# Attention and mixture of experts on one core: a reordered opening, later sums of V, and part of the early routing off VectorE

## The chip, the core and the metric

The kernel runs on one core of one Trainium2 chip. The metric is the time of one launch in microseconds (us), and of several runs the median. One further execution was taken by the hardware profiler; its trace is what the sections below quote.

## The reference, cut to what matters

```python
q_bits = (einsum('bhsd,dk->bhsk', q, proj) > 0)          # 6 sign bits per row of q, the same for k
mask   = q_bucket[:, :, :, None] == k_bucket[:, :, None, :]
scores = where(mask, q @ k.T / sqrt(64), -1e9)
attn   = exp(scores - scores.max(-1)); attn /= attn.sum(-1) + 1e-09
x      = (attn @ v) as 3072 tokens x 512                 # 4 batches, 8 heads, 768 rows, 64 columns
flat   = (x @ w_gate).flatten()                          # 3072 x 8 logits
for idx in argsort(-flat):                               # greedy: best logit first
    give token idx//8 to expert idx%8, unless the token has one or the expert has its 384
out    = per expert e: relu(x[mask_e] @ w1[e]) @ w2[e]   # 512 -> 1024 -> 512
```

## The kernel before, in words

There are 32 heads, taken in 8 groups of four; a group is two pairs of heads, and 128 partitions hold one pair (64 columns each). Every f32 operand is split into a f16 high half and a low half, so that TensorE multiplies in f16 and keeps the precision.

For each head TensorE works through three things. **Score passes** (`S_pass`, L233): for each of six blocks of 128 query rows, two matmuls against all keys, from the high halves and six rows of scaled sign bits, and one VectorE reduction (L241) for the row's maximum. Three maxima at a time are turned into a row (`m_rows`, L243: three short matmuls and one ScalarE step, L248), which becomes one more row of the operand `qa`; `qa` and `ka` hold the high halves, the sign bits and this row, and `qb` and `kb` the other halves. **Scores, transposed** (`ST`, L252): for each of six blocks of 128 keys, in two halves of 384 queries, matmuls L257 and L258 and an exponential on ScalarE (L259) into `pt`. **The product with V** (`AV`, L264), four steps behind: `pt`'s upper 16 bits against V's high and low half (L272, L273), and its low half `lo` (L274), which GpSimd or VectorE makes by a subtraction (L262). For rows whose bucket is empty the sum of V is needed (`sumv`, `sumw`, L194 to L213): matmuls of a column of ones against V's high and low halves (L203), a copy, a second matmul (L209) and a VectorE step into `wf`, with which the head's last product (L278, L279) is taken.

The main loop has 192 steps, one for each head and key block, in two half-steps each. What else a half-step does is fixed by hand in a table, `AP` (L20): `P1`, `P2`, `P3`, `P4` give, for group 1, 2, 3 and the later ones, the half-steps of the high halves (`cast`, L123), the low halves (`sub`, L129), the sign bits (`bits`, L131), the load of V and the sums of V (entry 18); `SU` is the half-step of group 0's sums, `SW` how much later `sumw` follows `sumv` in the later groups; `S` is the line by which score passes run ahead of the scores; `PAT`, `E0`, `E1` say which of a head's six `lo` go to VectorE. `MV` says when SP issues a group's moves into `qa`, `ka`, `qb`, `kb` (`moves`, L165) and, among them, the loads of the next group's q and k.

The **opening** is written out in the string `OPS`: its entries up to the first `|` run in that order ahead of the loop, and those behind belong to half-step 0, 1, and so on. A letter names a step (L319): `b` the projection of head 0's signs (`tbits`), `s` a score pass, `B` the sign bits of head 1 and of the pair of heads 2 and 3, `D` their two DMAs to head 1, `m` the row of maxima, `e` a first half of scores, `v` and `x` high and low half of V, `u` the low halves of pair 1, `r` and `l` head 0's and 1's other halves, `d` and `f` the moves of pair 1 (`dm`, L146, `dm2`, L158), `c` a cast, `C` copies into the second set of buffers, `w` dummy matmuls that keep TensorE busy. `DW[0]` dummies of 512 columns come before anything else. Steps of an engine are issued in the order of the program, so a step that waits holds up all that stand behind it on its engine.

In group 0's `bits` head 1 is read from XT with 64 of the 128 partitions and the pair from the loaded group with all 128; the result is scaled by 8192 on VectorE (L144), in later groups on ScalarE (`bscale`, L145).

After half of batch 3's attention, the **early routing** begins: the logits of the first three batches are known, and `early` (L536) hands out steps one by one, every four half-steps from half-step 307 (`EA`). For the first 18 of 24 columns of tokens, `best` (L485) finds each token's largest logit `m`, the expert it belongs to (`eq` times the weights `wt`, L495, then a maximum `mxu`), a sortable key, its first digit `E` and a one-hot of the expert (`OH`, L502). Three `compare` steps (L507) then set digits of six columns each against a table of 128 thresholds (L510). These run on VectorE, between the reductions of the score passes and the `lo` that fall to it.

The step that ends the early routing's part is followed by rounds of counting (from 395 us) and by the experts' matrix products, in which the change touches nothing.

## Time and profile before

| | |
|---|---|
| three runs | 734.71, 735.23 and 735.5 us, median 735.23 |
| profiled execution | 734.54 us, of which the trace's span is 732.8 |
| TensorE matmul busy | 673.7 us (92%) |
| VectorE busy | 519.3 us (71%) |
| ScalarE busy | 470.1 us (64%) |
| GpSimd busy | 525.4 us (72%) |
| mean granted TensorE clock | 0.97 |
| DMA | 93.58 MB in 39952 packets |

In the rows PE is TensorE's matmuls, PEld its weight loads, DVE VectorE, ACT ScalarE, POOL GpSimd and SP the queue that issues most DMAs. A row of a timeline gives the start in us from the span's start, the duration, the engine, the line, the operation, what it writes and reads, shapes and types, and in brackets how long the engine stood idle before and what ended that. A granted clock of 1.00 is TensorE's full speed, 2.4 GHz, and 0.50 half of it, 1.2 GHz. The attention loop ends at some 395 us. Shares over the whole span mix stages, so stages are read apart.

### The profile page before, as it was taken

To read this page: it belongs to the slowest core of one execution; us is meant where nothing else is said; L and a number is where in the kernel's file an instruction comes from. 1 tells how busy PE (TensorE), PEld (TensorE's weight loads), DVE (VectorE), ACT (ScalarE), POOL (GpSimd) and SP (SyncE) were. 2 spreads that over 40 slices of the span, in tenths; PEclk is the share of its full clock that TensorE was granted. 3 is DMA by queue.
4 is the path that set the end of the run, shared out by engine and by line. 5 is a ranking of instruction groups with operands and counts; after the bars stand their busy time and mean duration, and the time that the engine had idled before them with its cause. 6 is when DMAs were issued, how large, how long until landed. Compare 5 with 4: busy or idle time off the path is not lost. (4 is left out here: it accounts for less than half of the span.)

```text
span 732.8 us, 19247 instructions
## 1 busy us (share of the span) xinstructions
PE 673.7 (92%) x7865; PEld 433.4 (59%) x7865; DVE 519.3 (71%) x1124; ACT 470.1 (64%) x886; POOL 525.4 (72%) x486
## 2 busy tenths in 40 slices
PE   8899989999999999998997599989898989899995
PEld 2566656767767677676675464545454555545552
DVE  5868876878877878788965688697878787843120
ACT  7678776778978788776662172927373645556650
POOL 8589959998988979886772446575756473867761
PEclk9999999999999999999997599999999999999998
DMA  7638572726636255430000344435352526172601
GB/s 194 173 93 229 141 190 50 204 69 134 180 93 165 80 151 158 89 81 23 24 24 23 110 165 147 156 138 179 127 175 98 205 88 229 55 277 58 258 29 43
DMA packets 39952, 93.58 MB, mean 128 GB/s; under 512 B 4548, under 2 KB 30520, under 8 KB 37816
## 3 DMA queue, kind: packets, MB, share of 16 engines
...
q8 instruction: 61, 1.00, 0.6%
...
## 5 line engine op out<-in xcount | busy, mean ns | idle before, releaser
L262 POOL TENSOR_TENSOR lo<-pt 128x768 f16<-128x768 f32 x143 | 229.7, 1621 | 40.6 <-ACT pt L259 33.0
L259 ACT ACTIVATE pt<-pst 128x384 f32<-128x384 f32 x384 | 181.1, 491 | 72.9 <-PE pst L258 63.3
L241 DVE TENSOR_REDUCE m<-pss 128x1 f16<-128x770 f32 x192 | 182.0, 957 | 51.8 <-PE pss L239 50.6
L257 PE MATMUL pst<-qa,ka 128*128 128x384 f16 x384 | 126.1, 329 | 7.3 <-ACT qa L248 4.0
L258 PE MATMUL pst<-qb,kb 128*128 128x384 f16 x384 | 125.8, 328 | 0.0
L274 PE MATMUL psv<-vh,lo 128*128 128x65 f16 x1152 | 121.7, 194 | 3.2 <-POOL lo L262 3.2
L273 PE MATMUL psv<-vl,pt 128*128 128x64 f16 x1152 | 121.9, 193 | 0.0
L272 PE MATMUL psv<-vh,pt 128*128 128x65 f16 x1152 | 121.9, 195 | 0.0
L272 PEld LDWEIGHTS <-pt 128*128 128x128 bf16 x1152 | 107.3, 98 | 11.2 <-issue 3.5
L273 PEld LDWEIGHTS <-pt 128*128 128x128 bf16 x1152 | 106.3, 99 | 8.0 <-issue 0.2
L274 PEld LDWEIGHTS <-lo 128*128 128x128 f16 x1152 | 106.3, 98 | 3.5 <-POOL lo L262 3.5
L239 PE MATMUL pss<-ka,qa 128*128 128x385 f16 x384 | 95.0, 330 | 0.4 <-DVE m L241 0.3
L757 ACT ACTIVATE wh<-wf 128x1024 f16<-128x1024 f32 x64 | 67.0, 1051 | 36.6 <-DMA wf<-in_w_dram,zwidx 34.3
L775 POOL TENSOR_TENSOR wl<-wf,wh 128x512 f16<-128x512 f32 x76 | 85.9, 1147 | 0.0
L818 PEld LDWEIGHTS <-wh 128*128 128x128 f16 x512 | 47.9, 98 | 33.4 <-issue 3.4
L830 PEld LDWEIGHTS <-hh 128*128 128x128 f16 x384 | 36.2, 98 | 40.7 <-issue 3.2
L833 ACT ACTIVATE o<-po 128x512 f32<-128x512 f32 x24 | 14.3, 595 | 70.7 <-PE po L830 60.4
L766 ACT ACTIVATE wf<-wf 128x1024 f32<-128x1024 f32 x55 | 58.0, 1055 | 1.0
L262 DVE TENSOR_TENSOR lo<-pt 128x768 f16<-128x768 f32 x49 | 56.8, 1159 | 1.5 <-ACT pt L259 1.0
L821 DVE SCALAR_TENSOR_TENSOR hl<-px,hh 128x384 f16<-128x384 f32 x64 | 34.6, 551 | 30.6 <-ACT hh L820 29.9
L820 ACT ACTIVATE hh<-px 128x384 f16<-128x384 f32 x64 | 31.0, 484 | 37.6 <-PE px L818 34.0
L818 PE MATMUL px<-xh,wh 128*128 128x384 f16 x256 | 53.6, 326 | 1.1 <-DVE xl L794 0.8
...
## 6 DMA issues: line engine op xcount, KB each, us to landing
...
```

The lines of the kernel that those rows point to most:

```text
L239: T.matmul(ps[:,hf,0:HK],QA[u][:,j,qc*128:qc*128+128],KA[u][:,j,hf*HK:hf*HK+HK],start=True,stop=True)
L241: V.tensor_reduce(M6[h][:,qc:qc+1],ps[:,:,0:HK],axis=AX.XY,op=ALU.max,negate=True)
L257: T.matmul(ps[:,0:384],KA[u][:,j,kr],QA[u][:,j,r],start=True,stop=False)
L258: T.matmul(ps[:,0:384],KB[u][:,j,kr],QB[u][:,j,r],start=False,stop=True)
L259: A.activation(PT[h,kc][0][:,r],ps[:,0:384],AF.Exp,scale=0.125)
L262: eng.tensor_tensor(l,p,p.bitcast(BF)[:,1::2],op=ALU.subtract)
L272: T.matmul(av[:,c,:],ph[:,r],VH[u][:,j,kc,:],start=(kc==0 and c==0),stop=False,skip_group_check=True)
L273: T.matmul(av[:,c,0:64],ph[:,r],VL[u][:,j,kc,:],start=False,stop=False,skip_group_check=True)
L274: T.matmul(av[:,c,:],l[:,r],VH[u][:,j,kc,:],start=False,stop=False,skip_group_check=True)
L757: s.nc.scalar.mul(h[:,r],f[:,r],WSC)
L775: for _ in range(n): s.nc.gpsimd.tensor_tensor(*s.pend.pop(0)[1],op=ALU.subtract)
L818: T.matmul(p[:,0:384],a[:,o:o+128],b[:,d],start=n==0,stop=n==11)
```

## The change

In words:

- *Loads.* The second half of the first rows (`first(1,64)`) is loaded ahead of group 0's pair 1 and V.
- *Sign bits of the opening.* Head 1's are taken with all 128 partitions, so that four column groups run with the same number of rows. The scaling by 8192 is now ScalarE's (`a0`).
- *Order.* `OPS` is written anew: eight dummies of 512 columns instead of five, three score passes ahead of the key bits `B0`, and the first row of maxima, `m0`, right behind them; the low halves of pair 1 (`u0`, `u1`) move ahead of it, and the loads of group 1's q and k (`L0`, `L1`) ahead of pair 1's moves `d0`; V's high and low halves and `m1`, `m2` shift; a copy of one number of `ka` by GpSimd (`g0`) makes that engine wait for the key signs of head 0.
- *Score passes.* `S` goes from [7, 30] to [7, 7].
- *Sums.* Group 0's `sumv` moves from half-step 13 to 15 with `sumw` 2 behind instead of 3; group 1's from 46 to 50, group 2's from 72 to 74, and `sumw` in all later groups from 4 to 9 half-steps behind.
- *Low halves.* Heads 4, 7, 8 and 10 send one more of their six `lo` to VectorE (`XL`).
- *Early routing.* For the first 18 columns the product with `wt` moves to GpSimd, and the experts `mxu` and the digits `E` are copied through TensorE (a matmul with the identity, `lift`) into a bank of PSUM, from which the one-hot and the three comparisons read them. The identity `identb` is made earlier for that.

The diff, cut to its core:

```diff
- S=[7, 30],
- DW=[5, 0, 0, 0, 384],
+ S=[7, 7],
+ DW=[8, 0, 0, 0, 384],
...
- SW=4,
+ SW=9,
+ XL={4:[0,3,5],7:[1,4],8:[0,3,5],10:[0,3,5]},
...
- SU=13,
- OPS='b0 i3 i2 t0 b1 w5 r0 r2 w4 s0 w4 C1 r1 t1 c1 s1 B0 c0 D0 w2 w1 s4 w5 s2 s3 r3 v2 w5 v0 l0 l1 C0 m0 s5 w3 s6 r5 w2 l3 e0 e1 d0 u0 u1 s7 v1 l2 w0 m1 e2 | s8 | x0 | w0 | x1 s9 | r4 s10 | | | s11 m2 v3 f0 | x3 | | x2 | m3 | | | | | |')
+ SU=15,
+ OPS='b0 i3 i2 t0 w2 b1 w3 r0 r2 s0 w2 s1 C1 C0 r1 t1 c1 w4 s2 c0 w3 g0 l0 l1 u0 u1 B0 m0 a0 D0 s3 L0 L1 w2 e0 s4 d0 r3 l3 v2 v0 e1 w2 s5 e2 r5 l2 m1 s6 | s7 | x0 | s8 | v1 x1 | s9 | r4 s10 m2 | | s11 v3 f0 | x3 | | x2 m3 | | | | | |')
...
-    first(0,0); first(0,64); first(1,0)
+    first(0,0); first(0,64); first(1,0); first(1,64)
     for w,src in ((0,qT),(1,kT)): SY.dma_start(LD[0][w][:,1],src[0][:,1])
     SY.dma_start(LD[0][2],vv[0])
-    first(1,64)
...
-                    T.matmul(ps[32*w:32*w+32,hf,0:384],pr[0:64],(qd,kd)[w][0:64,1,hf*384:hf*384+384],start=True,stop=True,tile_position=(0,32*w))
+                    T.matmul(ps[32*w:32*w+32,hf,0:384],pr,(qd,kd)[w][:,1,hf*384:hf*384+384],start=True,stop=True,tile_position=(0,32*w))
...
-        if G==0: V.tensor_scalar(bt[r],bt[r],8192.0,None,op0=ALU.mult)
...
+        e=lambda k: ST(0,k,0),C=lambda n: copies((QA,KA)[n]),w=lambda n: warm(n,DW[4]),a=lambda n: bscale(0),
+        g=lambda n: G_.tensor_copy(tick,KA[0][64:65,0,0:1]))
...
-    add(AP['WS'],wsplit); add(AP['SU'],sumv,0); add(AP['SU']+3,sumw,0)
+    add(AP['WS'],wsplit); add(AP['SU'],sumv,0); add(AP['SU']+2,sumw,0)
...
-            if G==1 or w==2: add(p[19+w],load,G,w)
+            if w==2: add(p[19+w],load,G,w)
...
-            lambda: V.tensor_tensor(eq[:,r],eq[:,r],wt,op=ALU.mult),
+            lambda: W.tensor_tensor(eq[:,r],eq[:,r],wt,op=ALU.mult),
...
-            lambda: V.tensor_tensor(OH[:,r],bc(mxu),wt,op=ALU.is_equal)]
+            lambda: V.tensor_tensor(OH[:,r],s.lift(ps,mxu[:,r])[:,:,None].to_broadcast([128,n,8]) if ps else bc(mxu),wt,op=ALU.is_equal)]
+
+    def lift(s,ps,a):
+
+        g=ps()[:,0:a.shape[1]]
+        s.nc.tensor.matmul(g,s.identb,a,start=True,stop=True)
+        return g
...
+            if b==nb-2: todo.append(lambda a=a: s.compare(s.Z["cmp"][0],0,s.lift(ps,s.Z["E"][:,0,a:a+6]),a,a+6,a))
+            else: todo.append(lambda a=a: s.compare(s.Z["cmp"][0],0,s.Z["E"][:,0],a,a+6))
```

Lines of the changed kernel are shifted by one in attention and by up to nine in the routing. The order of the instructions shows the change at three places that matter for what follows.

The first is ScalarE in the opening, before. L248 is the row of maxima, L227 and L191 are casts (the rest of q and k, and V), L259 is an exponential.

```order
L127 CAST kh<-kp 128x768 [waits DMAHW7_49]
L127 CAST qh<-qp 128x768 [waits DMAHW6_49]
L227 CAST qb_175<-XT 64x768 [waits DMAHW1_49]
L191 CAST vh_211<-vp 128x6x64 [waits DMAHW0_49]
L191 CAST vh_211<-vp 128x6x64
L248 ACTIVATE qa_173<-pst,mbi,msc 32x384 [waits DVE_49,PE_49,Pool_49]
L227 CAST qb_175<-XT 64x768
L259 ACTIVATE pt<-pst 128x384 [waits PE_49] x2
L191 CAST vh_211<-vp 128x6x64
L248 ACTIVATE qa_173<-pst,mbi,msc 32x384 [waits PE_49]
```

And of the change, from the same two casts on:

```order
L128 CAST kh<-kp 128x768 [waits DMAHW1_49]
L128 CAST qh<-qp 128x768 [waits DMAHW0_49]
L248 ACTIVATE qa_176<-pst,mbi,msc 32x384 [waits DVE_49,PE_49,Pool_49]
L145 ACTIVATE bt<-bt 128x768 [waits DVE_49]
L259 ACTIVATE pt<-pst 128x384 [waits PE_49]
L227 CAST qb_178<-XT 64x768 [waits DMAHW6_49]
L191 CAST vh_214<-vp 128x6x64 [waits DMAHW2_49]
L191 CAST vh_214<-vp 128x6x64
L259 ACTIVATE pt<-pst 128x384 [waits PE_49] x2
L227 CAST qb_178<-XT 64x768
L248 ACTIVATE qa_176<-pst,mbi,msc 32x384 [waits PE_49]
```

The first row of maxima stands ahead of three casts that it followed; between it and the second stand the scaling, four casts and three exponentials, where there were two casts and two exponentials.

The second is SP's queue from head 1's sign rows (L316) on, before: the moves of pair 1 (L151) and its sign rows (L157) come ahead of the loads of group 1 (L61).

```order
L316 DMA ka_174<-bt 6x768 [waits DMAHW7_49]
L318 DMA qa_177<-qa_173 64x1536 [waits DMAHW0_49]
L318 DMA qa_177<-qa_173 64x1536 [waits DMAHW1_49]
L151 DMA qa_173<-qh 64x768 [waits DMAHW2_49,Activation_49]
L151 DMA ka_174<-kh 64x768 [waits DMAHW3_49]
L151 DMA qa_173<-qh 64x768 [waits DMAHW4_49]
L151 DMA ka_174<-kh 64x768 [waits DMAHW5_49]
L157 DMA qa_173<-bt 6x768 [waits DMAHW6_49,DMAHW1_49,DMAHW0_49]
L157 DMA ka_174<-bt 6x768 [waits DMAHW7_49]
L157 DMA qa_173<-bt 6x768
L157 DMA ka_174<-bt 6x768
L61 DMA qp<-in_qT_dram 128x1536 [waits DMAHW2_49,PE_49,Pool_49]
```

And of the change:

```order
L316 DMA qa_176<-bt 6x768 [waits DMAHW0_49,Activation_49]
L316 DMA ka_177<-bt 6x768 [waits DMAHW1_49]
L62 DMA qp<-in_qT_dram 128x1536 [waits DMAHW2_49,PE_49,Pool_49]
L62 DMA kp<-in_kT_dram 128x1536 [waits DMAHW3_49,PE_49,Pool_49]
L151 DMA qa_176<-qh 64x768 [waits DMAHW4_49]
L151 DMA ka_177<-kh 64x768 [waits DMAHW5_49]
L151 DMA qa_176<-qh 64x768 [waits DMAHW6_49]
L151 DMA ka_177<-kh 64x768 [waits DMAHW7_49]
L157 DMA qa_176<-bt 6x768 [waits DMAHW0_49]
L157 DMA ka_177<-bt 6x768 [waits DMAHW1_49]
L157 DMA qa_176<-bt 6x768 [waits DMAHW2_49]
L157 DMA ka_177<-bt 6x768 [waits DMAHW3_49]
```

Both loads, each with a wait for GpSimd (the last reader of the buffer is a low half of pair 1), now stand ahead of the eight moves of heads 2 and 3, and head 1's sign rows wait for ScalarE's scaling.

The third is VectorE in the early routing, before, from the one-hot (L502) to the first comparison (L510).

```order
L262 TENSOR_TENSOR lo<-pt 128x768 [waits Activation_49]
L502 TENSOR_TENSOR zOH<-zmxu,wt 128x144
L241 TENSOR_REDUCE m_7370<-pss 128x1 [waits PE_49]
L286 TENSOR_SCALAR r_7588<-psv 128x6 [waits PE_49]
L287 RECIPROCAL r_7588<-r_7588 128x6 [waits DVE_49]
L289 TENSOR_TENSOR X<-psv,r_7588 128x6x64 [waits DVE_49]
L241 TENSOR_REDUCE m_7599<-pss 128x1 [waits PE_49]
L510 TENSOR_TENSOR zcmp_390<-zE,tb_96 128x768
```

And of the change:

```order
L262 TENSOR_TENSOR lo<-pt 128x768 [waits Activation_49]
L503 TENSOR_TENSOR zOH<-pst,wt 128x144 [waits PE_49]
L241 TENSOR_REDUCE m_7362<-pss 128x1 [waits PE_49]
L286 TENSOR_SCALAR r_7582<-psv 128x6 [waits PE_49]
L287 RECIPROCAL r_7582<-r_7582 128x6 [waits DVE_49]
L289 TENSOR_TENSOR X<-psv,r_7582 128x6x64 [waits DVE_49]
L241 TENSOR_REDUCE m_7593<-pss 128x1 [waits PE_49]
L517 TENSOR_TENSOR zcmp_382<-pst,tb_96 128x768 [waits PE_49]
```

Both operations keep their place, read a bank of PSUM (`pst`) in place of a tile in SBUF, and wait for TensorE, which has written it.

## Rows read from the trace of the kernel before

**Rows 1.** Busy by stage: stretch, length, PE, PEld, DVE, ACT, POOL, clock, DMA, GB/s.
```profile
28.00:36.00 8.00, 5.88 (x75) 3.75 (x75) 6.68 (x8) 5.89 (x13) 8.00 (x7) 1.00 0.92 273
37.00:40.00 3.00, 3.00 (x31) 1.98 (x27) 0.96 (x1) 2.92 (x7) 3.00 (x3) 0.50 0.65 244
120.00:330.00 210.00, 206.65 (x3266) 150.71 (x3264) 168.56 (x231) 166.11 (x361) 189.92 (x163) 1.00 0.49 127
330.00:366.00 36.00, 32.59 (x501) 23.77 (x498) 32.84 (x47) 23.58 (x49) 23.90 (x15) 1.00 0.08 24
```

**Rows 2.** Timeline of TensorE: start, duration, step; its idle before in brackets.
```profile
25.52 0.32 PE L257 MATMUL pst<-qa,ka 128*128 128x384 f16 x1 [0.57 <-ACT qa L248]
...
33.47 0.28 PE L203 MATMUL pst<-vh,on 128*32 128x256 f16 x1
...
35.82 0.27 PE L203 MATMUL pst<-vl,on 128*32 128x256 f16 x1 [2.07 <-POOL vl L192]
...
70.28 0.27 PE L203 MATMUL pst<-vl,on 128*32 128x256 f16 x1 [1.70 <-POOL vl L192]
...
110.80 0.20 PE L274 MATMUL psv<-vh,lo 128*128 128x65 f16 x1 [3.16 <-POOL lo L262]
...
360.32 0.32 PE L257 MATMUL pst<-qa,ka 128*128 128x384 f16 x1 [1.35 <-DVE XT L301]
```

**Rows 3.** Timeline of TensorE in the opening.
```profile
5.14 5.28 PE L222 MATMUL pst<-XT,prt 64*6 64x384 f32 x8 [1.64 <-DMA prt<-in_proj_dram]
10.36 2.97 PE L75 MATMUL psv<-wrm 128*128 128x384 f16 x9
13.16 0.49 PE L239 MATMUL pss<-ka,qa 128*128 128x385 f16 x2
...
14.71 0.83 PE L138 MATMUL pss<-XT,pr 64*32 64x384 f32 x4
...
17.36 0.49 PE L142 MATMUL pss<-kp,pr 128*32 128x384 f32 x1
17.78 0.66 PE L75 MATMUL psv<-wrm 128*128 128x384 f16 x3
```

**Rows 4.** Timeline of TensorE: first and last of group 1's sign-bit matmuls.
```profile
46.66 0.51 PE L142 MATMUL pss<-qp,pr 128*32 128x384 f32 x1
...
47.67 0.49 PE L142 MATMUL pss<-kp,pr 128*32 128x384 f32 x1
```

**Rows 5.** The costliest groups: count, busy time, mean ns of one, idle before.
```profile
L259 ACT ACTIVATE pt<-pst 128x384 f32<-128x384 f32 x384 | 181.1, 491 | 72.9 <-PE pst L258 63.3
L241 DVE TENSOR_REDUCE m<-pss 128x1 f16<-128x770 f32 x192 | 182.0, 957 | 51.8 <-PE pss L239 50.6
```

**Rows 6.** Timeline of ScalarE in the opening.
```profile
21.76 0.66 ACT L248 ACTIVATE qa<-pst,mbi,msc 32x384 f16<-32x384 f32 x1 [5.97 <-issue]
22.45 0.83 ACT L227 CAST qb<-XT 64x768 f16<-64x768 f32 x1
...
24.80 0.66 ACT L248 ACTIVATE qa<-pst,mbi,msc 32x384 f16<-32x384 f32 x1
```

**Rows 7.** Timeline of GpSimd, at four places.
```profile
26.35 0.25 POOL L295 TENSOR_TENSOR wgs<-wgr,wgs 128x32 f16<-128x32 f32 x1 [8.55 <-issue]
...
33.27 2.49 POOL L192 TENSOR_TENSOR vl<-vp,vh 128x384 f16<-128x384 f32 x2
...
71.56 1.65 POOL L130 TENSOR_TENSOR ql<-qp,qh 128x768 f16<-128x768 f32 x1 [1.33 <-DMA qb<-ql]
...
107.68 1.64 POOL L130 TENSOR_TENSOR ql<-qp,qh 128x768 f16<-128x768 f32 x1 [7.92 <-DMA qb<-ql]
```

**Rows 8.** All DMA of the span.
```profile
DMA packets 39952, 93.58 MB, mean 128 GB/s; under 512 B 4548, under 2 KB 30520, under 8 KB 37816
```

**Rows 9.** Timeline of VectorE and GpSimd in the early routing.
```profile
333.47 1.61 DVE L495 TENSOR_TENSOR zeq<-zeq,wt 128x144 f32<-128x144 f32 x1
...
357.08 1.86 DVE L510 TENSOR_TENSOR zcmp<-zE,tb 128x768 bf16<-128x768 bf16 x1
...
361.52 0.55 DVE L510 TENSOR_TENSOR zcmp<-zE,tb 128x768 bf16<-128x768 bf16 x1
...
357.05 3.20 POOL L262 TENSOR_TENSOR lo<-pt 128x768 f16<-128x768 f32 x2 [1.20 <-ACT pt L259]
```

More of the change, by code (lines that the diff above doesn't have):

```diff
@@ L25 @@
  LEAD=9,
- S=[7, 30],
- DW=[5, 0, 0, 0, 384],
- P1=[13, 13, 14, 15, 17, 21, 23, 21, 16, 27, 21, 26, 23, 24, 33, 32, 3, 4, 46, -6, 3, 13],
- P2=[41, 44, 48, 49, 51, 51, 57, 55, 45, 49, 55, 57, 52, 60, 59, 60, 2, 3, 72, 32, 36, 47],
+ S=[7, 7],
+ DW=[8, 0, 0, 0, 384],
+ P1=[13, 13, 14, 15, 17, 21, 23, 21, 16, 27, 21, 26, 23, 24, 33, 32, 3, 4, 50, -6, 3, 13],
+ P2=[41, 44, 48, 49, 51, 51, 57, 55, 45, 49, 55, 57, 52, 60, 59, 60, 2, 3, 74, 32, 36, 47],
  P3=[69, 73, 82, 80, 84, 86, 89, 86, 75, 83, 87, 90, 94, 96, 97, 106, 2, 3, 122, 58, 62, 87],
@@ L119, in attention @@
         WF.append(cp.tile([128,4,65],F16,name=f"wf{u}")); G_.memset(WF[u],0.0)
+    tick=cp.tile([1,1],F32,name="tick")
     TMP={}
@@ L319, in attention @@
     OPS=dict(i=lambda j: init(j,A.copy),t=top,b=tbits,r=lambda n: rest(n//3,n%3),l=lambda n: rlo(n//2,n%2),
-        c=lambda w: cast(0,w,1),u=lambda w: sub(0,w,1),s=lambda k: S_pass(k//6,k%6),B=lambda n: bits(0,[1]),D=lambda n: bdma(),
+        c=lambda w: cast(0,w,1),L=lambda w: load(1,w),u=lambda w: sub(0,w,1),s=lambda k: S_pass(k//6,k%6),B=lambda n: bits(0,[1]),D=lambda n: bdma(),
         m=lambda n: m_rows(n//2,n%2),d=lambda n: dm(0,[1]),f=lambda n: dm2(0,[1]),v=lambda j: cv(0,j),x=lambda j: sv(0,j,G_),
-        e=lambda k: ST(0,k,0),C=lambda n: copies((QA,KA)[n]),w=lambda n: warm(n,DW[4]))
+        e=lambda k: ST(0,k,0),C=lambda n: copies((QA,KA)[n]),w=lambda n: warm(n,DW[4]),a=lambda n: bscale(0),
+        g=lambda n: G_.tensor_copy(tick,KA[0][64:65,0,0:1]))
     n=-1; early=[]
@@ L377, in attention @@
             hh,ss=divmod(t-1,6)
-            lo(hh,ss,V if ss in (E0 if hh<1 else E1 if hh<2 else PAT[hh%2]) or t==6*NH else G_)
+            lo(hh,ss,V if ss in (E0 if hh<1 else E1 if hh<2 else AP['XL'].get(hh,PAT[hh%2])) or t==6*NH else G_)
         run(2*t+1)
@@ L452, in consts @@
         s.hits=[fill([128,1],0.0,f"hit{i}",BF) for i in range(2)]; s.satl=fill([128,8],0.0,"satl",BF)
-        s.identb=cp.tile([128,128],BF,name="identb")
         s.gp=cp.tile([128,2,2,NC],BF,name="gp")
@@ L458, in consts @@
             todo.append(lambda i=i,v=v: A.activation(s.gp[:,i,1,:],pcol.to_broadcast([128,NC]),AF.Copy,scale=v))
+        s.identb=cp.tile([128,128],BF,name="identb")
+        todo.append(lambda: G_.tensor_scalar(s.identb,s.jp,0.0,None,op0=ALU.is_equal))
         s.th=iota([128,4,NC],[[128,4],[0,NC]],0,4097,name="th")
@@ L469, in consts @@
         s.rem=fill([128,8],float(s.CAP),"rem"); s.nrem=fill([128,8],-s.CAP/128.0,"nrem",F16)
-        todo.append(lambda: G_.tensor_scalar(s.identb,s.jp,0.0,None,op0=ALU.is_equal))
         s.nus=[col(-2.0**-sum(WID[:l+1]),f"nus{l}") for l in range(5)]
@@ L483, in ps, with best @@
     def ps(s): return s.psA.tile([128,512],F32,name="psa")
-    def best(s,P,c0,c1,first=False):
-        V=s.nc.vector; n=c1-c0; r=slice(c0,c1); L3=s.Lm[:,r]
+    def best(s,P,c0,c1,first=False,ps=None):
+        V=s.nc.vector; W=s.nc.gpsimd if ps else V; n=c1-c0; r=slice(c0,c1); L3=s.Lm[:,r]
         m,eq,mx,mxu,OH,key,D,E=(P[x] for x in ("m","eq","mx","mxu","OH","key","D","E"))
@@ L501, in best, with compare, paired @@
             lambda: V.tensor_tensor(E[:,0,r],D[:,0,r],s.sc[:,0,r],op=ALU.mult),
-            lambda: V.tensor_tensor(OH[:,r],bc(mxu),wt,op=ALU.is_equal)]
+            lambda: V.tensor_tensor(OH[:,r],s.lift(ps,mxu[:,r])[:,:,None].to_broadcast([128,n,8]) if ps else bc(mxu),wt,op=ALU.is_equal)]
[3 more added lines that the diff above has]
+        return g
     def digit(s,P,l,r):
         s.nc.vector.tensor_scalar(P["D"][:,l,r],P["key"][:,r],SH[l],(1<<WID[l])-1,op0=ALU.logical_shift_right,op1=ALU.bitwise_and)
-    def compare(s,cmp,l,d,c0=0,c1=None,eng=None):
+    def compare(s,cmp,l,d,c0=0,c1=None,off=0):
         J=NT[l]; tb=s.TB[l]
-        o,i,b=s.paired(d,c0,s.NC if c1 is None else c1,J,cmp,tb)
-        (eng or s.nc.vector).tensor_tensor(o,i,b,op=ALU.is_ge)
-    def paired(s,d,c0,c1,J,out,tb):
+        o,i,b=s.paired(d,c0,s.NC if c1 is None else c1,J,cmp,tb,off)
+        s.nc.vector.tensor_tensor(o,i,b,op=ALU.is_ge)
+    def paired(s,d,c0,c1,J,out,tb,off=0):
         r=slice(c0//2,c1//2); sh=[128,c1//2-c0//2,J,2]
-        return out[:,r],d[:,c0:c1].rearrange("p (s q) -> p s q",q=2)[:,:,None].to_broadcast(sh),tb[:,None].to_broadcast(sh)
+        return out[:,r],d[:,c0-off:c1-off].rearrange("p (s q) -> p s q",q=2)[:,:,None].to_broadcast(sh),tb[:,None].to_broadcast(sh)
     def count(s,pc,P,cmp,l,c0,c1):
@@ L545, in early @@
             s.Z["cmp"]=[s.z([128,NC//2,32 if i else NT[0],2],BF,f"cmp{i}",bufs=1) for i in range(3)]
-        todo=s.best(s.Z,c0,c0+n,True)
-        for a in range(c0,c0+n,6): todo.append(lambda a=a: s.compare(s.Z["cmp"][0],0,s.Z["E"][:,0],a,a+6))
+        todo=s.best(s.Z,c0,c0+n,True,ps if b==nb-2 else None)
+        for a in range(c0,c0+n,6):
+            if b==nb-2: todo.append(lambda a=a: s.compare(s.Z["cmp"][0],0,s.lift(ps,s.Z["E"][:,0,a:a+6]),a,a+6,a))
+            else: todo.append(lambda a=a: s.compare(s.Z["cmp"][0],0,s.Z["E"][:,0],a,a+6))
         if b==nb-1:
```

## The prediction

> **What bounds the kernel now.** I read the busy shares on the page first, then busy time by stage, then TensorE's idle times in order of time, then the rows around each. TensorE is the busiest engine, and the stages say where it isn't [rows 1]: from 120 to 330 us it is busy 206.65 of 210 us, so little off it can matter there; in 28 to 36 and in 330 to 366 it stands idle 2.1 and 3.4 us, and from 37 to 40 it is busy at a granted clock of 0.50. In 330 to 366 VectorE is busy 32.84 of 36 us. A change pays where TensorE starts earlier, where one of those idles shrinks, or where the clock stays up.
>
> The idles have names [rows 2]. At 25.52 the scores of the second query half wait for ScalarE's row of maxima; that step opens the steady loop. At 35.82 and 70.28 the sums of V of groups 0 and 1 wait 2.07 and 1.70 us for GpSimd's low halves. At 110.80 the attention product waits 3.16 us for GpSimd. At 360.32 TensorE waits 1.35 us for a PSUM bank that VectorE is late to empty. The 0.50 of 37 to 40 us comes right behind the wait at 35.82: TensorE's lower level, 1.2 GHz. Three us at half speed cost some 1.6.
>
> **The change part by part.** Durations are from the profiled execution, 734.5 us; it lies 0.7 under the median of 735.2, which I add at the end.
>
> *Opening.* Before, the projections for head 0's signs end at 10.42, nine dummy matmuls of 0.33 follow, and the first score pass starts at 13.16; the key bits of head 1 and pair 1 take from 14.71 to 17.85, 3.1 us [rows 3]. There, matmuls with 64 rows alternate with those with 128. The same work for group 1, all 128 rows in four column groups, ran from 46.66 to 48.16, 1.5 us [rows 4]; I take that for the new form (3.1 again if the groups don't overlap). After: two dummies between query and key signs let the projections end at 11.1; three more, to 12.05, cover the two VectorE steps that finish the key signs. Then three passes (0.66 at half clock, 0.33, 0.33) and nine dummies (1.5 at full clock) bring the bits to 14.9 to 16.4. Each pass needs VectorE 0.96 [rows 5]; three reductions end by 15.6, covered. ScalarE's first row of maxima followed the bits by as much as TensorE needs for three short matmuls, 0.4: 16.8 instead of 21.76 [rows 6]. But more stands on ScalarE between this row (0.66) and the second: the scaling by 8192 that left VectorE and two casts of 768 columns (0.83 each), two casts of V and three exponentials of 384 (0.49 each): 5.6 us, against 3.04 before. So the second row starts at 22.4 instead of 24.80, 2.4 earlier, and the loop opens at 23.1. One score pass fewer is done by then, 0.33 of TensorE still to pay: **-2.0**. Bounds: 0 if ScalarE queues further, -5 if all follows the first row. Dummies removed gain nothing of their own, TensorE waits there anyway.
>
> *The tick* makes GpSimd wait for the key signs, to about 12. Four subtractions of 1.64 [rows 7] end at 18.6; the first scores need two of them, 15.3, and wait for the row of maxima until 17.5. Price 0 under that cover, up to 1 without it.
>
> *Loads of group 1 ahead of the moves of heads 2 and 3.* SP issues two loads of 768 KB when the fourth subtraction is done and head 1's rows are out, at some 20.5. Head 2's moves and sign rows (0.4 MB) queue behind. At the 273 GB/s of 28 to 36 us [rows 1], in which just such loads and moves ran, that is 5.8 and 1.4 us, with about 2 to start and land: sign rows at 29 to 30. The new pass table begins head 2 two steps later, five steps into the loop; 6.5 steps took 7.95 before (25.52 to 33.47), so some 29. **+0.6**; bounds 0 and, at the page's mean of 128 GB/s [rows 8], +9.
>
> *Sums of group 0, two half-steps later.* GpSimd's chain from its first step in the loop (26.35) to the last low half took 9.4 us [rows 7]. It starts now when ScalarE has done the second row and a short cast, 23.3, and ends at 32.7; TensorE comes to the sums at 23.1+7.95 and one step of 1.6: 32.65. The wait of 2.07 shrinks to some 0.3 and the slow stretch behind it (1.6) goes. The second part of the sums is now one step behind the first, with the last product of head 0 right after; I charge 0.4. **-3.0**; bounds 0 and -3.7.
>
> *Sums of group 1, four half-steps later.* The 1.70 goes, but the scores of head 4, which stood behind it, need the low parts that SP moves; GpSimd's own wait on that transfer ended at 71.56 [rows 7], and TensorE will come to them near 69.4 of the old time, after the first of two pairs. I charge 0.4. **-1.3**; bounds 0 and -1.7. The wait at 110.80 stays: GpSimd waited there for a transfer until 107.68, and that chain starts with head 3's output.
>
> *One subtraction of heads 4, 7, 8, 10 each to VectorE*: 1.6 off GpSimd, about 1 on VectorE, in the stage where TensorE is busy 206.65 of 210. 0, bounds +1 and -1.
>
> *Early routing.* For VectorE the product with the weights took 1.61, two of the comparisons 1.86 and 0.55 [rows 9]. The 1.86 began 0.03 behind a GpSimd step; the same shape took 0.55 while GpSimd stood idle, so the long ones wait until GpSimd's step ends. The product goes to GpSimd, which has 12 of 36 us free [rows 1]. One-hot and comparisons now read one operand from PSUM, which GpSimd's steps don't touch: I take the 0.96 of the reduction over 770 PSUM elements for a comparison and 0.3 for the one-hot of 144, whose old form resembles the product. VectorE saves 1.6+1.3+0.5 = 3.4 of its 32.84. Of TensorE's 3.4 idle there I give it 1.9, and charge 0.4 for four short matmuls. **-1.5**; bounds -2.5 and +2, since each lifted copy holds one of three PSUM banks.
>
> The Trainium skill, "VectorE: DVE Perf Modes", section "Why PSUM operands drop a tier", speaks against this: an operand in PSUM holds a two-tensor operation to one element a cycle where 16-bit operands in SBUF run two. By that rule a comparison costs 0.4 more than the row of 0.55; if all three had run at 0.55, the term would be -0.7. The rows have one at 1.86, so I keep -1.5.
>
> Sum: -2.0+0.6-3.0-1.3-1.5 = -7.2; 734.5-7.2 = 727.3, with the 0.7 **728.0 us**.
>
> **The rivals.** *The clock rises in the opening* (0.12). Eight dummies of 512 columns stand ahead instead of five. In the rows the projections ran at 0.64 a pass and nine dummies at 0.33, three later ones at 0.16 to 0.17 [rows 3]: the lower level until about 13, after five. If eight lift it, the eight passes of 5.28 us take 2.6 less: 725.4. "TensorE: Matmul & The Clock Gate" of the Trainium skill, part 1, says that the clock is low by default and activity releases it; by that rule more dummies help.
>
> *The opening falls short* (0.18). TensorE waits for ScalarE from about 19 to 22.5 with few dummies left; a clock drop like the one at 37 costs 1.6, and head 2's rows may come 3 us late instead of 0.6: 728.0+1.6+2.4 = 732.0. For: ScalarE's longer chain. Against: no drop came behind the 1.70 at 70.
>
> *Given back at 108* (0.07). If the transfer that ended GpSimd's wait at 107.68 does not move, what was won before it only lengthens the 3.16: the 1.5 of the routing stays, with the 0.7 that is 733.7, no change. Against: SP's moves there follow head 3's output.
>
> *Slower* (0.07). The two loads block the ring. At 128 GB/s they take 12.3 us, the moves 3.1, and sign rows land at 38. Head 2's first pass, due at 29 at the head of TensorE's queue, waits 9 us, and the clock drops behind it (1.6): 728.0-0.6+9+1.6 = 738.0. It decides from a landing at some 36 us on. Against: the 273 GB/s.
>
> **How the numbers follow.** My forecast, 725.5 to 731 with all terms near their values, has 0.56. About 0.2%, 1.5 us, is what a measurement of this kernel tells from no change. Faster: 0.56, 0.12 and 0.17 of the short opening, 0.85; within 0.2%: the 0.07 and the last 0.01 of the short opening, 0.08; slower 0.07. The range, 723.5 to 733.5, leaves out the slower case and the one given back at 108, 0.14 together, and some 0.05 of the others past its two ends.
>
> **What would show it.** Right: the loop opens near 23.1 instead of 25.52; the bits take 1.5; no wait over 0.5 for low halves at the sums, and a granted clock of 1.00 in the steps behind them; head 2's first pass waits under 1; comparisons near 0.95, and under 2 us of TensorE idle in the 36 us of early routing. Wrong: a wait on a transfer at head 2, waits for VectorE at the four lifts, or an idle at 108 that grew by what was won before it.

## The result and the profile after

| | before | changed |
|---|---|---|
| median of 20 runs | 735.48 us (733.15 to 738.93) | 728.75 us (725.11 to 734.11) |
| profiled execution, and its span | 734.54, 732.8 | 725.11, 723.1 |
| busy PE, DVE, ACT, POOL | 673.7, 519.3, 470.1, 525.4 | 668.3, 529.5, 471.6, 520.3 |

The ratio of the runs is 0.9913, with a 95% interval of 0.9898 to 0.9928: some 6.4 us faster, and the forecast was 728.0. But the profiled execution of the changed kernel is the lowest of its 20 and lies 9.4 under that of before; a second profile of the same program, below, took 730.08. One run of the change, the one of 737.79 us in its repeat below, is in a slow state (a lower granted clock) and stays out of the ratio there. So the trace is read as one draw of several, and the parts of the change are compared in it place by place.

The page of the changed kernel, its first part:

```profile
span 723.1 us, 19219 instructions
...
PE 668.3 (92%) x7859; PEld 430.1 (59%) x7859; DVE 529.5 (73%) x1126; ACT 471.6 (65%) x887; POOL 520.3 (72%) x484
```

Busy time by stage, with the columns of [rows 1]; the last two stretches stand for its last two, 11 us earlier, though the last holds more matmuls (550 against 501):

```profile
28.00:36.00 8.00, 7.27 (x114) 4.81 (x113) 5.25 (x6) 6.58 (x16) 7.65 (x6) 1.00 0.60 175
36.00:40.00 4.00, 3.00 (x34) 1.91 (x32) 3.93 (x6) 3.24 (x8) 2.51 (x2) 1.00 0.00 0
40.00:44.00 4.00, 3.30 (x44) 1.71 (x44) 3.17 (x4) 1.67 (x3) 3.98 (x3) 1.00 0.41 102
...
109.00:319.00 210.00, 207.14 (x3244) 149.59 (x3243) 176.04 (x233) 165.58 (x360) 186.15 (x161) 1.00 0.49 127
319.00:355.00 36.00, 35.02 (x550) 26.02 (x547) 33.66 (x47) 24.62 (x51) 25.88 (x17) 1.00 0.09 24
```

In the early routing TensorE's idle in 36 us has gone from 3.4 to 1.0 us (from the mark of head 25 to that of head 31, which are explained below and bound the same work, from 3.7 to 2.3); the stretch at half clock behind the first sums is gone; and there is a new hole, 1.0 us idle in 36 to 40 and 0.7 in 40 to 44. TensorE's timeline names the places; these rows answer to [rows 2 to 4]:

```profile
5.17 1.45 PE L222 MATMUL pst<-XT,prt 64*6 64x384 f32 x4 [0.54 <-DMA prt<-in_proj_dram]
9.60 0.49 PE L239 MATMUL pss<-ka,qa 128*128 128x385 f16 x2 [0.57 <-DVE ka L224]
12.15 0.51 PE L143 MATMUL pss<-qp,pr 128*32 128x384 f32 x1
...
13.20 0.49 PE L143 MATMUL pss<-kp,pr 128*32 128x384 f32 x1
...
20.12 0.32 PE L257 MATMUL pst<-qa,ka 128*128 128x384 f16 x1 [0.58 <-ACT qa L248]
...
30.24 0.28 PE L203 MATMUL pst<-vl,on 128*32 128x256 f16 x1
...
40.70 0.49 PE L239 MATMUL pss<-ka,qa 128*128 128x385 f16 x2 [1.70 <-DVE m L241]
...
67.38 0.28 PE L203 MATMUL pst<-vl,on 128*32 128x256 f16 x1
...
101.30 0.20 PE L274 MATMUL psv<-vh,lo 128*128 128x65 f16 x1 [0.21 <-POOL lo L262]
```

Half of the projections take 1.45 us, where all eight passes took 5.28: they ran at the higher level. The key bits go from 12.15 to 13.69, 1.5 us. The loop opens at 20.12 instead of 25.52. Both sums stand without a bracket, so without a wait. At 101.30, where 3.16 us were lost before, 0.21 are. The 1.70 at 40.70 is new. ScalarE's two rows of maxima are 5.36 us apart, 3.04 before [rows 6]:

```profile
14.05 0.66 ACT L248 ACTIVATE qa<-pst,mbi,msc 32x384 f16<-32x384 f32 x1 [0.30 <-issue]
14.74 0.84 ACT L145 ACTIVATE bt<-bt 128x768 f16<-128x768 f16 x1
...
19.41 0.66 ACT L248 ACTIVATE qa<-pst,mbi,msc 32x384 f16<-32x384 f32 x1
```

VectorE and GpSimd in the early routing, answering to [rows 9]:

```profile
342.36 0.30 DVE L503 TENSOR_TENSOR zOH<-pst,wt 128x144 bf16<-128x144 f32 x1
345.19 0.95 DVE L517 TENSOR_TENSOR zcmp<-pst,tb 128x768 bf16<-128x768 f32 x1
348.72 0.95 DVE L517 TENSOR_TENSOR zcmp<-pst,tb 128x768 bf16<-128x768 f32 x1
353.49 0.94 DVE L517 TENSOR_TENSOR zcmp<-pst,tb 128x768 bf16<-128x768 f32 x1
...
322.22 0.49 POOL L496 TENSOR_TENSOR zeq<-zeq,wt 128x144 f32<-128x144 f32 x1
```

The comparisons are even, as forecast, and the product that took VectorE 1.61 takes GpSimd 0.49.

### The profile page after: what moved, and what is told of

It reads as the page before. It is cut to its first block, busy times and chain, and to the rows that moved or that the text cites. A ratio compares the mean times of both kernels' runs of the same rounds, so it can differ in the third digit from the quotient of the medians.

```text
span 723.1 us, 19219 instructions
## 1 busy us (share of the span) xinstructions
PE 668.3 (92%) x7859; PEld 430.1 (59%) x7859; DVE 529.5 (73%) x1126; ACT 471.6 (65%) x887; POOL 520.3 (72%) x484
## 5 line engine op out<-in xcount | busy, mean ns | idle before, releaser
L262 POOL TENSOR_TENSOR lo<-pt 128x768 f16<-128x768 f32 x139 | 225.1, 1632 | 45.0 <-ACT pt L259 40.7
L259 ACT ACTIVATE pt<-pst 128x384 f32<-128x384 f32 x384 | 181.5, 492 | 69.7 <-PE pst L258 57.3
L262 DVE TENSOR_TENSOR lo<-pt 128x768 f16<-128x768 f32 x53 | 72.1, 1360 | 2.0 <-ACT pt L259 1.5
```

The lines of the kernel that those rows point to most:

```text
L259: A.activation(PT[h,kc][0][:,r],ps[:,0:384],AF.Exp,scale=0.125)
L262: eng.tensor_tensor(l,p,p.bitcast(BF)[:,1::2],op=ALU.subtract)
```

## The experiments

All were timed beside the kernel before on the same chip; a ratio is to that kernel, with its 95% interval. Since whole times of one program spread over up to 12 us, the profiles are compared at marks: the second scores row (the loop opens) and VectorE's first step on the output of a head (line 286, at 43.02 for head 0 and 392.16 for head 31 in the kernel before). Differences to the kernel before in us, minus is earlier:

| profile | loop opens | head 0 | head 2 | head 3 | head 6 | head 25 | head 31 | span |
|---|---|---|---|---|---|---|---|---|
| the change | -5.4 | -7.1 | -4.7 | -7.3 | -10.0 | -10.1 | -11.0 | -9.7 |
| the change again | -2.0 | -3.5 | -1.0 | -3.0 | -4.0 | -4.1 | -5.0 | -4.7 |
| five dummies | -0.5 | -2.0 | 0.5 | -1.4 | -3.5 | -3.5 | -4.4 | -5.2 |
| sums back | -5.4 | -8.1 | -5.7 | -7.0 | -6.1 | -6.1 | -8.1 | -10.3 |
| routing back | -5.5 | -7.2 | -4.8 | -7.1 | -9.2 | -9.3 | -8.6 | -9.2 |
| opening only | -5.4 | -8.3 | -5.8 | -7.1 | -6.8 | -7.1 | -7.1 | -6.9 |
| first sums back | -5.1 | -6.8 | -4.3 | -6.4 | -8.3 | -8.4 | -9.4 | -8.5 |
| loads back | -5.4 | -6.0 | -3.6 | -6.0 | -7.9 | -8.0 | -9.0 | -9.0 |
| twelve dummies | -4.8 | -6.8 | -4.3 | -5.5 | -7.1 | -7.2 | -8.2 | -9.0 |
| before, eight dummies | 0.4 | -0.5 | -0.5 | -1.0 | -2.1 | -1.2 | -1.2 | 0.0 |
| before, two low buffers | 4.7 | 4.6 | 4.6 | 4.0 | -0.4 | -1.1 | -1.1 | -0.7 |
| first sums back, two low buffers | -5.4 | -8.0 | -5.5 | -7.6 | -11.0 | -11.5 | -12.5 | -13.2 |
| the same instructions again (the last run below) | -5.4 | -8.2 | -5.7 | -9.0 | -12.4 | -12.9 | -13.8 | -14.2 |

**The change once more.** No edit.

> The change itself once more, for a second profile of the same program. If its attention part is the same from run to run and the spread of 725 to 734 comes from the routing and the experts behind it, head 31's last output falls again 11.0 us earlier than in the kernel before, within 1. If the spread comes from the transfers around 80 to 105 us (the rival), the wait for GpSimd's low half that followed the move of ql is 0.2 in one profile and 1 to 3 in the other, with a granted clock of 0.50 behind it where it is over 2.

Measured: 729.08 us (725.28 to 737.79), ratio 0.9908 (0.9882 to 0.9933); the profiled execution 730.08. Neither expectation alone: at head 31 it is 5.0 ahead of before, not 11.0, and most of the 6.0 between the two profiles of one program is there when the loop opens, 3.4 us, and at head 0, 3.7. TensorE in this profile:

```profile
5.19 2.72 PE L222 MATMUL pst<-XT,prt 64*6 64x384 f32 x4 [0.40 <-DMA prt<-in_proj_dram]
...
12.45 0.80 PE L239 MATMUL pss<-ka,qa 128*128 128x385 f16 x2
13.67 0.49 PE L239 MATMUL pss<-ka,qa 128*128 128x385 f16 x2
...
23.52 0.32 PE L257 MATMUL pst<-qa,ka 128*128 128x384 f16 x1 [0.75 <-ACT qa L248]
...
107.36 0.20 PE L274 MATMUL psv<-vh,lo 128*128 128x65 f16 x1 [1.94 <-POOL lo L262]
```

```profile
24.00:27.00 3.00, 3.00 (x11) 1.35 (x9) 2.23 (x3) 1.78 (x4) 3.00 (x4) 0.50 0.99 319
```

The projections ran at half the rate (2.72 for what took 1.45) and the clock was up only between the passes of 12.45 and 13.67. The loop then opens at 23.52; the prediction, which had taken the low level until about 13, said 23.1. Right behind the opening the granted clock is 0.50 for 3 us, the drop that the prediction's rival of a short opening names; it cost little, for from the loop's opening to head 0 this profile gains 1.5 us on the kernel before and the first one 1.7. The wait for GpSimd's low half is 1.94 here, 0.21 in the first profile: the transfers that it hangs on vary too.

**Five dummies.**

```diff
- DW=[8, 0, 0, 0, 384],
+ DW=[5, 0, 0, 0, 384],
```

> The change with five dummies of 512 columns at the very start instead of eight, nothing else undone. The prediction's forecast case: the dummies do nothing, TensorE only waits there; the projections run at 0.64 a pass in both kernels, the time stays within 1 us of the change's 728.75, and the loop opens near 23.1. The rival (eight dummies lift the clock): the profile of the change shows the first four projections in 1.45 us instead of 2.6, and the first score pass at 9.60 instead of 13.16; with five they take 0.64 a pass again, the first pass starts 2.6 to 3.5 later, the loop opens at 23 to 24 instead of 20.12, and the time is 2.5 to 3.5 above the change, 731 to 732.

Measured: 728.54 us (724.83 to 731.63), ratio 0.9916 (0.9888 to 0.9943). The profile goes with the rival: 2.72 for four projections, loop open at 25.06. The times do not: they are the change's. Over all profiles, with eight dummies or more the projections ran at the higher level in nine of eleven, with five in none of three; but that a run without a profile gains by the three more dummies is not shown.

**Eight dummies alone, in the kernel before.**

```diff
- DW=[5, 0, 0, 0, 384],
+ DW=[8, 0, 0, 0, 384],
```

> The kernel before with eight dummies of 512 columns at the start instead of five, nothing else. The theory that the three more dummies lift the clock: the eight passes of the projections take some 2.9 us instead of 5.28 and the first score pass starts near 10.5 instead of 13.16; what of it reaches the loop is bounded by ScalarE's row, which stands behind casts of loaded data: 0 to 2.5 us earlier opening than 25.52, 0 to 2.5 off the time. The rival (the new order is needed for it too): projections at 0.64 a pass, no change.

Measured: 731.93 us (729.23 to 736.32), ratio 0.9968 (0.9950 to 0.9986); in the profile the clock stayed low here too, and nothing opened earlier:

```profile
5.18 5.28 PE L222 MATMUL pst<-XT,prt 64*6 64x384 f32 x8 [0.40 <-DMA prt<-in_proj_dram]
...
13.24 0.84 PE L239 MATMUL pss<-ka,qa 128*128 128x385 f16 x2
...
36.24 0.27 PE L203 MATMUL pst<-vl,on 128*32 128x256 f16 x1 [2.07 <-POOL vl L192]
...
110.11 0.20 PE L274 MATMUL psv<-vh,lo 128*128 128x65 f16 x1 [2.34 <-POOL lo L262]
```

```profile
36.00:40.00 4.00, 3.76 (x62) 2.81 (x62) 1.17 (x2) 3.03 (x7) 4.00 (x4) 1.00 0.86 262
112.00:116.00 4.00, 3.92 (x78) 3.01 (x74) 3.55 (x4) 3.92 (x10) 4.00 (x3) 1.00 0.02 4
```

The ratio says that three dummies are worth 1 to 3.7 us in the kernel before; in this profile they were not, at the opening. The profile tells something else: the wait of 2.07 at group 0's sums is the same as in the kernel before, but the granted clock behind it stays at 1.00, and head 0 comes 0.9 earlier against the loop's opening. So the half clock does not follow from that wait alone, and it is worth 0.9 us, not the 1.6 that the prediction charged. Behind the 2.34 at 110.11 the clock stays up too.

**Twelve dummies.**

```diff
- DW=[8, 0, 0, 0, 384],
+ DW=[12, 0, 0, 0, 384],
```

> The change with twelve dummies of 512 columns at the start instead of eight. In the profiles with eight the clock was up at the projections (four in 1.45 to 1.79 us) in five of seven and only near 13 us in two; with five in none of three. The theory that a longer run of full matmuls lifts it more surely: projections at the high clock in this profile, fewer runs above 730, median up to 1 us below the change's. Against it: twelve end near 6 us where the clock stays low, so the projections start 0.4 to 0.9 later than 5.2, and the time is the same or 0.5 longer.

Measured: 726.05 us (724.57 to 728.93), ratio 0.9901 (0.9875 to 0.9927). The clock was up at the projections (four in 1.45 us), which started 0.6 later (5.81), and no run lies over 729, where 7 of the change's 25 lie over 730 (737.79 left out). The interval overlaps the change's, so this points one way and settles nothing.

**All sums of V back.** Also entry 18 of `P1` from 50 to 46 and of `P2` from 74 to 72.

```diff
- SW=9,
+ SW=4,
- SU=15,
+ SU=13,
-    add(AP['SU']+2,sumw,0)
+    add(AP['SU']+3,sumw,0)
```

> The change with all sums of V where they were before (group 0 at half-steps 13 and 16, group 1 at 46, group 2 at 72, sumw 4 behind sumv). The prediction: 3.0 and 1.3 come back, 4.3 in all, 733; a wait of some 2 us for GpSimd's low half at group 0's sums with a granted clock of 0.50 behind it, and 1.7 at group 1's. The rival: the new opening starts GpSimd's chain in the loop 5.9 us earlier (20.45 instead of 26.35) and the opening of the loop 5.4 earlier, so the low halves are done at 29.1 against sums that stand at some 28.6: group 0's wait is 0.5 and the clock holds; only group 1's 1.7 comes back, 730 to 731.

Measured: 724.61 us (724.47 to 724.90, four runs), ratio 0.9867 (0.9845 to 0.9889): faster, not slower. Rows of TensorE, and by stage:

```profile
28.73 0.28 PE L203 MATMUL pst<-vh,on 128*32 128x256 f16 x1
29.13 0.27 PE L203 MATMUL pst<-vl,on 128*32 128x256 f16 x1
...
63.89 0.27 PE L203 MATMUL pst<-vl,on 128*32 128x256 f16 x1 [0.96 <-POOL vl L192]
...
103.80 0.24 PE L274 MATMUL psv<-vh,lo 128*128 128x65 f16 x1 [2.12 <-POOL lo L262]
```

```profile
104.00:108.00 4.00, 4.00 (x47) 2.78 (x45) 1.82 (x2) 2.04 (x4) 4.00 (x4) 0.64 0.00 0
```

Three things follow. Group 0's sums do not wait at their old place in the new opening (no bracket at 29.13), and head 0 is 1.0 earlier than with the move. Group 1's wait is back, 0.96, and from head 2 to head 3 the change gains 2.7 where this kernel gains 1.3. And at 103.80 TensorE waits 2.12 us for the low half, with a granted clock of 0.64 behind it: from head 5 to head 6 the change gains 3.05, this kernel 0.1. Up to head 31 the change is 2.9 ahead of it. Its runs are nevertheless below the change's, and the intervals do not meet. In the profiles that comes from behind attention, where this one gains 2.2 us between head 31 and the end and the change loses 1.3; why, and whether it would hold over more than four runs, stays open. So no whole time shows a gain from the moved sums.

**Group 0's sums alone back.**

```diff
- SU=15,
+ SU=13,
-    add(AP['SU']+2,sumw,0)
+    add(AP['SU']+3,sumw,0)
```

> The change with group 0's sums of V alone back at half-steps 13 and 16; the later groups' sums stay moved. The prediction: the 3.0 of this term come back, slower. From the profiles of the change and of all sums back: head 0's output comes 1.0 us earlier with the old place and keeps that until head 2, since GpSimd's low halves are done at 29.1 in the new opening and TensorE does not wait for them; 1.0 faster at head 31's output than the change, 12.0 ahead of the kernel before.

Measured: 729.88 us (725.06 to 734.26), ratio 0.9929 (0.9903 to 0.9955). Missed: head 0 is not earlier here. Head 2's first pass waited 1.29 us for a sign row in this profile, which is more than the 1.0 that is missing:

```profile
27.60 0.49 PE L239 MATMUL pss<-ka,qa 128*128 128x385 f16 x2 [1.29 <-DMA ka<-bt]
```

In the four other profiles with these sums at their old place (all sums back, the opening alone, and the last two rows of the table) head 0 is 8.0 to 8.3 ahead, against the change's 7.1.

**Early routing back.** Lifts and the product on GpSimd undone.

```diff
-        todo=s.best(s.Z,c0,c0+n,True,ps if b==nb-2 else None)
+        todo=s.best(s.Z,c0,c0+n,True,None)
-            if b==nb-2: todo.append(lambda a=a: s.compare(s.Z["cmp"][0],0,s.lift(ps,s.Z["E"][:,0,a:a+6]),a,a+6,a))
-            else: todo.append(lambda a=a: s.compare(s.Z["cmp"][0],0,s.Z["E"][:,0],a,a+6))
+            todo.append(lambda a=a: s.compare(s.Z["cmp"][0],0,s.Z["E"][:,0],a,a+6))
```

> The change with the early routing as before: product with wt on VectorE, one-hot and comparisons from SBUF, no matmul with the identity. The prediction: 1.5 come back (bounds 0.5 above none to 2.5), 730.2, and TensorE's idle from 20 us before to 45 us behind the start of that stage is 3.4 again instead of 1.8. The rival that this part is given back later (TensorE or VectorE ends the stage at the same time whatever the routing does): no change, 728.7 within 0.5.

Measured: 727.00 us (724.58 to 730.44), ratio 0.9908 (0.9881 to 0.9936). The waits are back in TensorE's timeline:

```profile
346.91 0.23 PE L247 MATMUL pst<-ident,m 128*128 128x128 f16 x1 [1.60 <-DVE m L241]
...
351.77 0.32 PE L257 MATMUL pst<-qa,ka 128*128 128x384 f16 x1 [1.34 <-DVE XT L301]
```

From head 25 to 31 this kernel loses 0.73 where the change gains 0.95: the part is worth 1.7 us in attention, forecast 1.5. With the sums at their old places it is worth 2.1 (all sums back gains 2.06 there, the opening alone, below, 0.00). The same four profiles show a price of the later sums: with them moved this stretch is 0.7 (routing as before) or 1.1 (new routing) longer (the low halves in which the profiles also differ end with head 10). So of the routing's 1.7 to 2.1 the change keeps 0.95 against the kernel before. In the whole time the part is not seen, for the interval is 4 us wide.

**The opening alone.** The edits of "all sums of V back" and of "early routing back", and

```diff
- XL={4:[0,3,5],7:[1,4],8:[0,3,5],10:[0,3,5]},
+ XL={},
```

> The change's opening, loads and line of score passes alone: sums where they were before, early routing as before, no extra subtractions on VectorE. The prediction's terms: -2.0 +0.6 = -1.4 against the kernel before, 734. The rival that the clock rises in the opening: -5 to -7 at the end of head 0, of which the wait at group 1's sums and the routing's idles take nothing: 729 to 731.

Measured: 729.82 us (724.87 to 732.89), ratio 0.9930 (0.9904 to 0.9956), inside the rival's 729 to 731. Head 0 is 8.3 earlier: the opening by itself takes the loop's 5.4 and then the 2.07 wait and the half clock at group 0's sums, 2.9 more. It also tells of the low halves of heads 4, 7, 8 and 10: between heads 9 and 10 every profile with them on VectorE loses 0.95 to 1.1, this one nothing. From there to head 25 all sums back, which has them too, wins 0.38 and this kernel 0.37, so the loss stays; the 0.7 to 0.8 that the others win there goes with the moved sums.

**Loads back.** `L0 L1` taken out of `OPS` as well, so that group 1's loads stand again at half-steps -6 and 3.

```diff
-            if w==2: add(p[19+w],load,G,w)
+            if G==1 or w==2: add(p[19+w],load,G,w)
```

> The change with the loads of group 1's q and k behind the moves of heads 2 and 3, as before (half-steps -6 and 3). The prediction's term: +0.6 for the loads ahead, since head 2's sign rows land late; so 0.6 faster, and the waits of 0.23 to 1.29 us at head 2's first score pass, put down to a sign row in two of the profiles, go. The rival: ScalarE's casts of group 1 then wait for the loads (they waited 1.10 at 30.41 in the change with loads ahead), some 3 to 5 us longer, and the exponentials behind them; TensorE stands idle 2 us or more near 32 us, slower by 1 to 3 us.

Measured: 728.62 us (725.81 to 731.20), ratio 0.9938 (0.9914 to 0.9962). The loop opens at the same time, and head 0 is 1.1 later than in the change, head 3 1.4. ScalarE, then TensorE:

```profile
31.52 0.92 ACT L129 CAST qh<-qp 128x384 f16<-128x384 f32 x2 [2.58 <-DMA kb<-kl]
```

```profile
32.88 0.32 PE L257 MATMUL pst<-qa,ka 128*128 128x384 f16 x1 [1.83 <-ACT pt L259]
```

In the change ScalarE waited 1.10 there (at 30.41). So by these profiles the loads ahead are a gain: group 1's casts stand in front of exponentials that free TensorE's banks. The whole times do not show it, for the two intervals overlap.

**Two buffers for the low halves, in the kernel before.**

```diff
-            TMP[G,'l']=[dp.tile([128,2,S],F16,name=n,bufs=1) for n in ("ql","kl")]
+            TMP[G,'l']=[dp.tile([128,2,S],F16,name=n,bufs=2) for n in ("ql","kl")]
```

> The kernel before with two buffers each for the low halves of q and k instead of one, so that group 3's subtraction does not wait for the move of group 2's. The theory that the 3.16 us at 110.80 come from that transfer and the granted clock of 0.57 from 112 to 116 from the wait: both go, 3 to 4.5 us at head 7's output and at the end of attention, 731 to 732. The rival (GpSimd is late there anyway): the wait stays over 1.5 and the time within 1 of the kernel before.

Measured: 730.28 us (728.86 to 738.37), ratio 0.9953 (0.9930 to 0.9976). GpSimd's subtraction comes without a wait, and the wait of 3.16 and the half clock behind it are gone:

```profile
104.31 1.65 POOL L130 TENSOR_TENSOR ql<-qp,qh 128x768 f16<-128x768 f32 x1
```

```profile
112.00:116.00 4.00, 4.00 (x73) 3.13 (x71) 3.51 (x5) 3.59 (x9) 3.83 (x3) 1.00 0.48 184
```

From head 5 to head 6 it gains 5.7 us on the kernel before, whose clock fell there, and 3.5 on the one with eight dummies, whose clock did not. What the profile does not give to the time, it lost in the opening, by 4.7:

```profile
8.95 0.87 DVE L224 TENSOR_SCALAR qa<-qa 6x768 f16<-6x768 f16 x1
...
11.51 4.71 DVE L224 TENSOR_SCALAR ka<-ka 6x768 f16<-6x768 f16 x1
```

```profile
16.36 0.63 PE L239 MATMUL pss<-ka,qa 128*128 128x385 f16 x2 [2.77 <-DVE ka L224]
```

The scaling of head 0's key signs took 4.71 us: four GpSimd steps stood back to back from 9.68 to 16.0, and VectorE came through behind them. In the kernel before and in the one with eight dummies the same four steps stood there, and the scaling took 0.43 and 0.44. The change's tick makes GpSimd wait for exactly this result, and in all eleven profiles with it the scaling took 0.35; no run has the changed opening without the tick, so what it is worth is not shown.

**Both together: group 0's sums back and two low buffers,** in the changed kernel.

```diff
- SU=15,
+ SU=13,
-    add(AP['SU']+2,sumw,0)
+    add(AP['SU']+3,sumw,0)
-            TMP[G,'l']=[dp.tile([128,2,S],F16,name=n,bufs=1) for n in ("ql","kl")]
+            TMP[G,'l']=[dp.tile([128,2,S],F16,name=n,bufs=2) for n in ("ql","kl")]
```

> The change with group 0's sums of V back at their old place and two buffers for the low halves of q and k. In the kernel before, the second buffer took away the wait of 3.16 us and the half clock behind it, 5.7 us at head 6's output. In the change that wait was 0.21 in one profile and 1.94 in the other: it goes in all runs, worth 0.2 to 3 us; group 0's sums gain 1.0 more where the clock is up early. Expected: no wait over 0.3 for a low half between 95 and 120 us, the time at 0.987 to 0.989 of the kernel before (the change: 0.9908 to 0.9913). Against it: the wait is a matter of chance that the second buffer does not touch, ratio 0.991.

Measured: **721.57 us** (720.43 to 724.07), ratio 0.9844 (0.9820 to 0.9868), faster than both kernels; the intervals of this one and of the change do not meet. No wait for a low half is left between 95 and 120 us, and head 31 is 12.5 ahead of the kernel before. The run with group 0's sums alone back lacks only the second buffer (ratio 0.9929), and those intervals do not meet either.

**Head 1's fourth low half to GpSimd,** in the kernel just shown.

```diff
- E1=[3, 4],
+ E1=[4],
```

> The kernel of the run before the last two (group 0's sums back, two buffers for the low halves) with one more edit: the low half of head 1's fourth key block goes to GpSimd instead of VectorE. Every profile with the new opening shows one wait of 1.70 us near 40 us, where a score pass waits for VectorE's reductions, which stand behind that subtraction; it took 2.13 us there, for it began 0.16 behind a GpSimd step of 1.47. If that is the cause, the 1.70 goes and head 1's output comes 1 to 1.7 earlier, 720 or 0.982 to 0.983 of the kernel before. Against it: GpSimd, 1.47 later, then holds up the next group's low halves or head 1's product, and the wait only moves: 721.6 within 0.7.

Measured: 721.86 us (720.61 to 725.79), ratio 0.9852 (0.9823 to 0.9881). The edit does nothing: a later table of the routing bears the same name and is the one that the loop reads (its only entry from 0 to 5 is 2), so the instructions are the same as in the run before it, and the entry `E1` of `AP` decides nothing in either kernel. It serves as its repeat (twelve runs, 720.4 to 725.8). What the 1.70 at 40 us come from stays untested.

## Why the prediction was right, and where its steps were not

The forecast of 728.0 met the median of 728.75, but the terms that make it up did not all hold, and it was met between two kinds of execution; that it lies so near is in part luck. In the case that the prediction reckoned with (clock low until 13 us) the profile was 730.08, 4.5 under that of before against a forecast of 7.2; in the other, 725.11.

- *Opening, -2.0.* Right in the case it assumed: 23.52 for 23.1, key bits 1.5 for 1.5, ScalarE's chain 5.4 for 5.6. In most profiles the rival came true instead (the clock up at the projections): it was given 0.12 and 2.6 us, and brings 3.4 (20.12 against 23.52). The other rival, a short opening, came true in part beside it: a half clock from 24 to 27 us, which cost some 0.3 by head 0 and not 1.6.
- *The tick, 0.* The price of 0 stands: no wait of TensorE in the changed opening is put down to GpSimd. What the step left out is what it may save: VectorE's scaling took 0.43 in the trace of before, and that the same step can stand behind GpSimd for 4.71 us was not in that trace. The Trainium skill, "SBUF — State Buffer", section "Who interferes with whom", says that VectorE and GpSimd share one pair of ports as an exclusive lock; the 4.71 agrees, and it did not happen in two other profiles with the same steps (0.43 and 0.44). So "Price 0" is the step that is incomplete: it has no gain, which in an execution like that one would be up to 4.7.
- *Loads ahead, +0.6.* Wrong in sign: -1.1 at head 0 and -1.4 at head 3 by the run that undoes it. I counted the moves that queue behind the loads, and not ScalarE's casts that wait for the loads, nor the exponentials behind those casts. Head 2's rows were late in some profiles as forecast (waits of 0.35 to 1.29 us in four), under 0.3 in the others.
- *Sums of group 0, -3.0.* The size is right, and in part by luck; the cause is not. The wait and the slow stretch go, but by the new opening alone (2.9 in the run with only it), since GpSimd's chain starts as much earlier as TensorE. I let it start at 23.3 and end at 32.7; even with the clock low its last low half was done at 32.45, and the sums at their old place, one step of 1.6 before 34.35, would by this estimate not have waited. The slow stretch was charged 1.6 and is worth 0.9, and by the prediction's own two times (32.7 and 32.65) the wait left would have been under 0.1, not 0.3. The move itself cost 1.0 where the profiles compare.
- *Sums of group 1, -1.3.* Measured 1.35 in the first pair of profiles (2.68 against 1.33 from head 2 to head 3), but -0.1 to 1.9 over the nine with these sums moved, for the low parts, charged at 0.4, cost 0.2 to 1.9 of waiting in eight of them. Not foreseen is that the later sums cost 0.7 to 1.1 between heads 25 and 31. The sums were 4.3 of the 7.2; with all of them back the time was not 733 but 724.61.
- *"The wait at 110.80 stays."* Wrong. In the four profiles with the old places it is 2.12 to 3.16; in the seven with the later groups' sums moved and one buffer it is 0.21 to 1.94. That the wait hangs on the buffer of the low half, which is still being moved out, is shown (a second buffer takes it away, in both kernels); why it is shorter with the moved sums is not settled.
- *Low halves of four heads, 0.* Mis-sized: 1.0 lost between heads 9 and 10, and 0.9 up to head 25 between all sums back and the opening alone, at the edge of the bound of +1. Between the marks of heads 9 and 10 VectorE is busy 12.9 of 14.1 us in the change, 10.3 of 13.1 in the opening alone; no run takes these halves alone back.
- *Early routing, -1.5.* Measured 1.7 to 2.1, with comparisons at 0.95 as taken and VectorE's saving 3.4 as summed (1.61, 1.27 at the one-hot, 0.52 at three comparisons); the later sums take 0.7 to 1.1 of it back. The side sum for three comparisons at 0.55 comes to some -0.5 by its own steps, not -0.7.
- *Not foreseen.* The 1.70 at 40.70, in every profile with the new opening. VectorE's reduction stands there behind a low half of 2.13 us that began 0.16 behind a GpSimd step of 1.47; that this is the cause is argued, not shown. And 1.3 us given back behind attention, where nothing was edited; profiles differ by 3.5 us there, from -2.2 to +1.3. In the change TensorE waited for ScalarE's copy of gathered tokens, where before it waited 0.29; of the other profiles only one has such a wait there (2.44):

```profile
414.25 1.44 PE L827 MATMUL px<-xh,wh 128*128 128x384 f16 x4 [2.59 <-ACT xh L814]
```
